# Local-plus-pooled attention and a gated feed-forward on one core: one PSUM read of h, attention groups behind the first product, second product two steps behind

## The chip, the cores and the metric

The kernel runs on one core of one Trainium2 chip. The metric is device time in microseconds (us) of one execution; the median of three runs before the change is 961.98 us (961.03 to 962.47).

## The reference, cut to what matters

For 8 batches, 8 heads, 576 positions and head size 64, two attentions are computed from q, k, v and added; the sum is the input of a feed-forward of width 512 to 2048 to 512.

```python
out_d  = softmax(scale * mean4(q) @ mean4(k).T) @ mean4(v)   # pooled by 4, 144 positions
out_up = np.repeat(out_d, 4, axis=2)
mask   = np.abs(pos[:, None] - pos[None, :]) < 4             # local band
x      = out_up + softmax(where(mask, scale * q @ k.T, -1e9)) @ v   # 4608 tokens x 512
h = x @ w_in                                                 # 512 -> 2048
g = np.where(h >= 1, h, np.where(h <= -1, 0.0, (h + 1) ** 2 / 4))
return g @ w_out                                             # 2048 -> 512
```

## The kernel before, in words

**Feed-forward.** The 4608 tokens are cut into 11 chunks: one of 512, eight of 384 (the middle chunks), two of 512. The 2048 hidden features are 16 slices of 128. A step n is one chunk and one slice (n = 16 * chunk + slice), so there are 176 steps. In each step `mm1` (L651) makes the first product: 12 matmuls (L659) into one PSUM bank `h_ps`. Each operand is split in a high and a low part (`xh`, `xl`; two planes of `w_in`), three matmuls for each of four 128-row blocks. Then `mm1` computes the activation g(h) into `u` and splits it as well: `gh` by a ScalarE cast (L683), `gl = u - gh` by GpSimd (L684). The `mm2` of a step (L687) adds the slice to the chunk's outputs: 9 matmuls (L700) into three PSUM banks `o_ps` for a middle chunk (12 into four for a chunk of 512), and copies the outputs out after slice 15 (L705, L707).

**Activation before.** In the first chunk it takes h from PSUM twice on VectorE (L672, L674). In all others ScalarE reads h (L677: relu of h/2 + 1/2), VectorE reads h (L678: max(h, 1) into `m`), ScalarE squares `u` (L679), VectorE takes the minimum (L680).

**Attention.** One unit is a pair of heads of one batch, 32 units in all. Eight of them are made before and during the first chunk by `attention` (L171). The other 24 are made in the middle chunks by the generator `join` (L393), 25 calls of it at the steps that `JOINS` lists (17, 20, 23, 26, 30, 37, 44, ... 137, 142). One call has four stages:

- stage 1, PE: the output matmuls of the unit before (L418, L433) and the scores of this unit (L447, L457), in one tile `join_ps` of four banks; SyncE issues the loads of q, k and v (L150, L156);
- stage 2: ScalarE scales the pooled output `xd` (L472); VectorE adds the band to the scores (L478) and takes maxima (L484, L495, L496, L497); GpSimd subtracts the maximum (L485); ScalarE takes exponentials of the local scores (L507) and of the three pooled blocks (L499 three times); VectorE adds local and pooled output of the unit before into `x` (L510), which ScalarE and GpSimd split into `xh`, `xl` (L379, L380);
- stage 3: VectorE sums, inverts, normalises (L522 to L528); GpSimd pools v (L535, L536); SyncE loads pooled v (L153);
- stage 4: PE transposes the weights ("the turns" below; L547 reads `sp` of L528, L553 reads `sl` of L525) into `turn_ps`, ScalarE copies them out (L557, L561), and VectorE pools the next q and k (L389), each after its load.

**Order of the work.** The code calls stages and products in program order, and a scheduler then sets a fixed order of instructions on each engine from priorities (the activation is called with a raised one, L667) and its own estimate of times. Each engine takes its own list strictly in order. In the middle chunks four banks hold `join_ps` or `turn_ps`, three hold `o_ps`, and one is left for `h_ps`: the first product of a step can start only when h of the step before has been read. `gh` and `gl` have three buffers each, `u`, `m` and the output copies share four.

Before the change a middle step n is (L725 to L735): stages 1 and 2 of a join if n is in `JOINS`, else stage 3 or 4 of the one begun a step or two ago; then mm1 of n; then mm2 of n - 1.

Of the kernel before, what the change touches and what calls it, by code (L numbers as in the profile page):

```python
# [13 lines left out]
AF = mybir.ActivationFunctionType  # L14
ALU = mybir.AluOpType
# [11 lines left out]
NFC = DFF // P  # L27
# [12 lines left out]
def ring(t):  # L40

    return (t - 512) % RING
# [60 lines left out]
JOINS = [17, 20, 23, 26, 30, 37, 44, 51, 58, 65, 69, 73, 78, 84, 91, 98, 105, 113, 117, 121, 125]  # L103
# [15 lines left out]
def attention_then_ffn(ctx: ExitStack, tc, qT, kT, vw, vp, band, w_in, w_out, out):  # L119
    nc = tc.nc  # L120
# [264 lines left out]
    def pooled_sums(n):  # L385

        state["qd"], state["kd"] = first_qd, apool.tile([P, SD], F32, name="kd", tag="kd", bufs=1)
        for t, name in ((first_qd[:, 0:SD], "q"), (state["kd"], "k")):
            nc.vector.tensor_reduce(  # L389
                t, loaded[name].rearrange("p (s f) -> p s f", f=FACTOR), axis=AX.X, op=ALU.add  # L390
            )
# [183 lines left out]
    def temp(name):  # L575
        return mpool.tile([P, 512], F32, name=name, tag="t512", bufs=4)

    def convert_weights(name, f):
# [26 lines left out]
    todo = {  # L605
        "w": iter(range(NFC)),
        "c": iter([(name, f) for f in range(NFC) for name in ("i", "o")]),
    }
    attentions = {}

    def emit(op):
        kind, n = op[0], int(op[1:] or 0)
        if kind == "a":
            if n not in attentions:
                attentions[n] = attention(n, ps_p if n < NPAIR else ps_a)
            next(attentions[n], None)
        elif kind == "c":
            convert_weights(*next(todo["c"]))
        elif kind == "w":
            load_weights(next(todo["w"]))  # L620
        elif kind == "q":
            nc.sync.dma_start(qk[n][0], qT[0, n])
            nc.sync.dma_start(qk[n][1], kT[0, n])
        elif kind == "v":
            load(0, "vp")
            load(0, "v")
        elif kind == "s":
            mm1(*next(todo["s"]))
        elif kind == "m":
            mm2(*next(todo["m"]))  # L630
# [16 lines left out]
    def turns(x):  # L647

        return x.rearrange("p (a b) -> p b a", a=2)

    def mm1(c, f):  # L651
        t0, size = CHUNKS[c]
        ts = slice(ring(t0), ring(t0) + size)
        wi = weights["i", f]
        h = places["h"].tile([P, 512], F32, name="h_ps", tag="h")[:, :size]
        n = 0
        for cc in range(NCC):
            for wt, xt in ((0, xh), (1, xh), (0, xl)):
                nc.tensor.matmul(  # L659
                    h,  # L660
                    wi[:, wt, cc * P : (cc + 1) * P],
                    turns(xt[:, cc, ts]),
                    start=(n == 0),
                    stop=(n == 3 * NCC - 1),
                )
                n += 1
        with tc.high_priority(offset=100):  # L667
            u = temp("u")[:, :size]


            if c == 0:
                nc.vector.tensor_scalar(u, h, -1.0, 1.0, op0=ALU.max, op1=ALU.add)  # L672
                nc.scalar.activation(u, u, AF.Square, scale=0.5)
                nc.vector.scalar_tensor_tensor(u, h, 1.0, u, op0=ALU.max, op1=ALU.min)  # L674
            else:
                m = temp("m")[:, :size]
                nc.scalar.activation(u, h, AF.Relu, bias=0.5, scale=0.5)  # L677
                nc.vector.tensor_scalar(m, h, 1.0, None, op0=ALU.max)  # L678
                nc.scalar.activation(u, u, AF.Square)  # L679
                nc.vector.tensor_tensor(u, u, m, op=ALU.min)  # L680
            gh = mpool.tile([P, 512], F32R, name="gh", tag="gh", bufs=3)[:, :size]
            gl = mpool.tile([P, 512], F32R, name="gl", tag="gl", bufs=3)[:, :size]
            nc.scalar.copy(gh, u)  # L683
            nc.gpsimd.tensor_tensor(gl, u, gh, op=ALU.subtract)  # L684
        gtiles[c, f] = gh, gl

    def mm2(c, f):  # L687
        t0, size = CHUNKS[c]
        gh, gl = gtiles.pop((c, f))
        if f == 0:  # L690
            otiles[c] = [
                (ps_o if t < 3 else places["o3"]).tile([P, 512], F32, name=f"o_ps{t}", tag=f"o{t}")
                for t in range(size // P)
            ]
        wo = weights["o", f]
        for t in (3, 0, 1, 2) if size == 512 else (0, 1, 2):
            o = otiles[c][t]
            ts = slice(t * P, (t + 1) * P)
            for n, (gt, wt) in enumerate(((gh, 0), (gh, 1), (gl, 0))):
                nc.tensor.matmul(  # L700
                    o, gt[:, ts], turns(wo[:, wt, :]), start=f == 0 and n == 0, stop=f == NFC - 1 and n == 2
                )
            if f == NFC - 1:
                osb = temp("osb")
                nc.scalar.copy(osb, o)  # L705
                rows = out[t0 : t0 + size, :].rearrange("(a b) d -> b a d", a=2)
                nc.sync.dma_start(rows[t * P // 2 : (t + 1) * P // 2], osb)  # L707
# [3 lines left out]
    with (  # L711
        tc.tile_pool(name="ps_o3", bufs=1, space=bass.MemoryType.PSUM) as places["o3"],
        tc.tile_pool(name="ps_h2", bufs=1, space=bass.MemoryType.PSUM) as ps_h2,
        tc.tile_pool(name="ps_a", bufs=1, space=bass.MemoryType.PSUM) as ps_a,
    ):
        places["h"] = Rotation(ps_h, ps_h2)
        for op in FIRST_STEPS:
            emit(op)
        mm1(*next(todo["s"]))
        mm2(*next(todo["m"]))  # L720
    with tc.tile_pool(name="ps_g", bufs=1, space=bass.MemoryType.PSUM) as ps_g:
        places["h"] = ps_h
        pooled_sums(SECOND)
        joined = None
        for n in range(NFC + 1, (NMID + 1) * NFC + 1):  # L725
            if n in JOINS:
                joined = join(SECOND + JOINS.index(n), ps_g)
                next(joined, None)
                next(joined, None)
            elif n - 1 in JOINS:  # L730
                next(joined, None)
            elif n - 2 in JOINS:
                next(joined, None)
            mm1(*next(todo["s"]))
            mm2(*next(todo["m"]))  # L735
    with (
        tc.tile_pool(name="ps_o3", bufs=1, space=bass.MemoryType.PSUM) as places["o3"],
        tc.tile_pool(name="ps_h2", bufs=1, space=bass.MemoryType.PSUM) as ps_h2,
# [63 lines left out]
```

## Time and profile before

| what | value |
|---|---|
| median of 3 runs | 961.98 us |
| the profiled execution's own time | 961.12 us |
| its span (first to last instruction) | 959.4 us |
| PE busy | 902.7 us, 94% |
| VectorE, ScalarE, GpSimd busy | 479.3, 473.1, 378.4 us |
| granted TensorE clock, mean | 0.982 |

The page gives busy time for each engine. PE is busy nearly throughout, but the end of a matmul is modelled, so a busy PE may still be short of work for a fraction of a microsecond. The timeline has one row for each group of like instructions: start and length in us, engine, line, operation, tiles out<-in, shape, count, and in brackets the engine's idle time before it with what ended it. A negative time below is a time ahead of the moment that is called zero there.

### The profile page before, as it was taken

The numbers are of one execution on the slowest core, as the hardware profiler recorded it, in microseconds if no ns is written. First come the engines' busy times: TensorE is split into PE (matmuls) and PEld (weight loads), VectorE is DVE, ScalarE is ACT, GpSimd is POOL, SyncE is SP. The second block draws the span as 40 slices with busy tenths as digits, with TensorE's granted clock in tenths as the row PEclk, the third lists the DMA queues.
The fourth block names the chain that finished last, engine by engine and source line by source line (L and its number), as shares of the span: only waits on it lengthen the run. The fifth ranks groups of instructions, "written<-read, shape, count | busy, mean of one in ns | idle before, by whom it ended". The sixth has DMA issues, their size and how long they took to land. (4 is left out here: it accounts for less than half of the span.)

```text
span 959.4 us, 18205 instructions
## 1 busy us (share of the span) xinstructions
PE 902.7 (94%) x7420; PEld 793.9 (83%) x7420; DVE 479.3 (50%) x836; ACT 473.1 (49%) x1011; POOL 378.4 (39%) x345
## 2 busy tenths in 40 slices
PE   4678999998999999999999999999999999999997
PEld 4556777887889888988889889988888888888886
DVE  5877797466443554355544553455556432222221
ACT  3898554445543544445444453454454443334333
POOL 2556666344443344344333443343444422222222
PEclk8689999999999999999999999999999999999999
DMA  9685110231220211132120121021231000001001
GB/s 313 223 305 206 51 53 26 72 101 52 74 63 13 72 52 52 41 88 60 51 68 18 52 84 32 21 85 52 73 115 52 15 7 27 1 1 45 1 1 44
DMA packets 26531, 66.21 MB, mean 69 GB/s; under 512 B 3152, under 2 KB 3152, under 8 KB 26448
## 3 DMA queue, kind: packets, MB, share of 16 engines
q1 hardware_dynamic: 26448, 65.06, 20.9%
q8 instruction: 58, 0.95, 0.4%
q14 instruction: 25, 0.20, 0.1%
HBM read 55.61 MB, written 9.44 MB: 68 GB/s over the span
## 5 line engine op out<-in xcount | busy, mean ns | idle before, releaser
L659 PE MATMUL h_ps<-xh,w_i 128*128 128x384 f32 (+1 forms) x1408 | 370.9, 345 | 17.2 <-DVE m L678 15.8
L684 POOL TENSOR_TENSOR gl<-u,gh 128x384 fp32r<-128x384 f32 (+1 forms) x176 | 192.2, 1092 | 452.1 <-ACT gh L683 337.8
L700 PE MATMUL o_ps<-w_o,gh 128*128 128x512 f32 x1152 | 349.5, 382 | 0.5 <-ACT gh L683 0.4
L659 PEld LDWEIGHTS h_ps<-xh,w_i 128*128 128x128 f32 x1408 | 251.7, 189 | 46.6 <-DVE m L678 25.5
L678 DVE TENSOR_SCALAR m<-h_ps 128x384 f32<-128x384 f32 (+1 forms) x160 | 93.3, 583 | 310.9 <-ACT u L677 301.9
L659 PE MATMUL h_ps<-xl,w_i 128*128 128x384 f32 (+1 forms) x704 | 240.0, 341 | 0.0
L700 PEld LDWEIGHTS o_ps<-w_o,gh 128*128 128x128 f32 x1152 | 214.5, 190 | 25.9 <-ACT gh L683 1.1
L700 PE MATMUL o_ps<-w_o,gl 128*128 128x512 f32 x576 | 220.1, 382 | 4.7 <-POOL gl L684 4.7
L677 ACT ACTIVATE u<-h_ps 128x384 f32<-128x384 f32 (+1 forms) x160 | 81.9, 512 | 225.0 <-PE h_ps L659 224.0
L683 ACT CAST gh<-u 128x384 fp32r<-128x384 f32 (+1 forms) x176 | 95.7, 544 | 107.4 <-DVE u L680 102.8
L659 PEld LDWEIGHTS h_ps<-xl,w_i 128*128 128x128 f32 x704 | 133.1, 189 | 5.4 <-issue 0.4
L700 PEld LDWEIGHTS o_ps<-w_o,gl 128*128 128x128 f32 x576 | 109.3, 190 | 22.2 <-POOL gl L684 6.9
L680 DVE TENSOR_TENSOR u<-u,m 128x384 f32<-128x384 f32 (+1 forms) x160 | 94.8, 592 | 13.6 <-ACT osb L705 0.5
L679 ACT ACTIVATE u<-u 128x384 f32<-128x384 f32 (+1 forms) x160 | 87.6, 547 | 4.7
L380 POOL TENSOR_TENSOR xl<-x,xh 128x576 fp32r<-128x576 f32 (+6 forms) x44 | 48.1, 1101 | 48.4 <-ACT xh L379 48.4
L478 DVE TENSOR_TENSOR sl<-join_ps,band_sb 128x640 f32<-128x640 f32 x24 | 19.8, 825 | 71.3 <-ACT xd L472 69.3
L485 POOL TENSOR_TENSOR sl<-sl,mxl 128x640 f32<-128x640 f32 x24 | 30.3, 1262 | 23.2 <-DVE mxl L484 23.2
L379 ACT CAST xh<-x 128x576 fp32r<-128x576 f32 (+6 forms) x44 | 23.7, 543 | 28.2 <-DVE x L510 23.7
L535 POOL TENSOR_TENSOR vh<-vp_sb 72x512 f32<-72x512 f32 x24 | 30.7, 1280 | 2.5 <-PE join_ps L433 2.5
L389 DVE TENSOR_REDUCE first_qd<-q_sb 128x144 f32<-128x576 f32 x24 | 18.1, 754 | 27.1 <-DMA q_sb<-qT 27.1
L593 POOL TENSOR_TENSOR w_i<-m,w_i 128x512 fp32r<-128x512 f32 x16 | 23.4, 1463 | 18.6 <-ACT w_i L592 18.4
L472 ACT ACTIVATE xd<-join_ps 128x144 f32<-128x144 f32 x24 | 7.0, 291 | 46.7 <-PE join_ps L457 45.8
(103 smaller groups left out, 841.7 us busy)
## 6 DMA issues: line engine op xcount, KB each, us to landing
v_sb<-vw SPq DMA_DIRECT2D x32, 320.0 KB
vp_sb<-vp SPq DMA_DIRECT2D x32, 288.0 KB
out<-osb SPq DMA_DIRECT2D x36, 256.0 KB
raw_i<-w_in SPq DMA_DIRECT2D x16, 512.0 KB
raw_o<-w_out SPq DMA_DIRECT2D x16, 512.0 KB
q_sb<-qT SPq DMA_DIRECT2D x28, 288.0 KB
k_sb<-kT SPq DMA_DIRECT2D x28, 288.0 KB
first_i<-qT SPq DMA_DIRECT2D x4, 288.0 KB
```

The lines of the kernel that those rows point to most:

```text
L379: nc.scalar.copy(xh[:, p, dst], x[:, part])
L380: nc.gpsimd.tensor_tensor(xl[:, p, dst], x[:, part], xh[:, p, dst], op=ALU.subtract)
L485: nc.gpsimd.tensor_tensor(slf, slf, ml.unsqueeze(2).broadcast_to([P, NB, WIN]), op=ALU.subtract)
L535: nc.gpsimd.tensor_tensor(vh, vpt[:, :, 0:2, :], vpt[:, :, 2:4, :], op=ALU.add)
L659: nc.tensor.matmul(h, wi[:, wt, cc * P : (cc + 1) * P], turns(xt[:, cc, ts]), start=(n == 0), stop=(n == 3 * NCC - 1),)
L677: nc.scalar.activation(u, h, AF.Relu, bias=0.5, scale=0.5)
L678: nc.vector.tensor_scalar(m, h, 1.0, None, op0=ALU.max)
L679: nc.scalar.activation(u, u, AF.Square)
L680: nc.vector.tensor_tensor(u, u, m, op=ALU.min)
L683: nc.scalar.copy(gh, u)
L684: nc.gpsimd.tensor_tensor(gl, u, gh, op=ALU.subtract)
L700: nc.tensor.matmul(o, gt[:, ts], turns(wo[:, wt, :]), start=f == 0 and n == 0, stop=f == NFC - 1 and n == 2)
```

## The change

Three things are changed, the first in `mm1`, the others in the loop over the middle steps.

- In every chunk but the first, h is read from PSUM once, by a ScalarE copy into `m`. VectorE then computes `u = max(m, -1) + 1` from SBUF, ScalarE squares u/2, and VectorE takes min(max(m, 1), u).
- In a middle step mm1 of n is called first, and the stages of a join behind it.
- mm2 is called two steps behind mm1 instead of one; step 17 has none, and one more follows the loop.

```diff
-                nc.scalar.activation(u, h, AF.Relu, bias=0.5, scale=0.5)
-                nc.vector.tensor_scalar(m, h, 1.0, None, op0=ALU.max)
-                nc.scalar.activation(u, u, AF.Square)
-                nc.vector.tensor_tensor(u, u, m, op=ALU.min)
+                nc.scalar.copy(m, h)
+                nc.vector.tensor_scalar(u, m, -1.0, 1.0, op0=ALU.max, op1=ALU.add)
+                nc.scalar.activation(u, u, AF.Square, scale=0.5)
+                nc.vector.scalar_tensor_tensor(u, m, 1.0, u, op0=ALU.max, op1=ALU.min)
...
         for n in range(NFC + 1, (NMID + 1) * NFC + 1):
+            mm1(*next(todo["s"]))
             if n in JOINS:
                 joined = join(SECOND + JOINS.index(n), ps_g)
+                next(joined)
                 next(joined, None)
+            elif n - 1 in JOINS or n - 2 in JOINS:
                 next(joined, None)
-            elif n - 1 in JOINS:
-                next(joined, None)
-            elif n - 2 in JOINS:
-                next(joined, None)
-            mm1(*next(todo["s"]))
-            mm2(*next(todo["m"]))
+            if n > NFC + 1:
+                mm2(*next(todo["m"]))
+        mm2(*next(todo["m"]))
```

The four lines of the activation keep their numbers (L677 to L680). What the scheduler makes of it is shown at the join of step 44; numbers in names tell buffers apart.

ScalarE around that join, before. `u_3487` belongs to step 44, `u_3530` to step 45:

```order
L472 ACTIVATE xd_3452<-join_ps_3395 128x144
L677 ACTIVATE u_3487<-h_ps_3474 128x384
L679 ACTIVATE u_3487<-u_3487 128x384
L507 ACTIVATE sl_3454<-sl_3454 128x640
L499 ACTIVATE sp_3459,join_ps_3395<-join_ps_3395,mxp_3460 128x144
L683 CAST gh_3493<-u_3487 128x384
L499 ACTIVATE sp_3459,join_ps_3395<-join_ps_3395,mxp_3460 128x144 x2
L379 CAST xh_80<-x_3468 128x320
L677 ACTIVATE u_3530<-h_ps_3517 128x384
```

ScalarE there now. `m_3400`, `u_3399` belong to step 44, `m_3511`, `u_3510` to step 45:

```order
L677 COPY m_3400<-h_ps_3386 128x384
L679 ACTIVATE u_3399<-u_3399 128x384
L683 CAST gh_3405<-u_3399 128x384
L472 ACTIVATE xd_3466<-join_ps_3409 128x144
L507 ACTIVATE sl_3468<-sl_3468 128x640
L499 ACTIVATE sp_3473,join_ps_3409<-join_ps_3409,mxp_3474 128x144 x2
L677 COPY m_3511<-h_ps_3497 128x384
L499 ACTIVATE sp_3473,join_ps_3409<-join_ps_3409,mxp_3474 128x144
L679 ACTIVATE u_3510<-u_3510 128x384
L379 CAST xh_80<-x_3482 128x320
```

The whole activation of step 44, its cast `gh` included, now stands ahead of `xd`, the first instruction of the join; the copy of step 45's h stands ahead of the third exponential.

VectorE from the pooling of q to the last instruction that the turns wait for (L528), before:

```order
L389 TENSOR_REDUCE first_qd_78<-q_sb_3446 128x144
L510 TENSOR_TENSOR x_3468<-join_ps_3395,xd_3452 128x576
L522 TENSOR_REDUCE join_ps_3395<-sl_3454 128x10
L389 TENSOR_REDUCE kd_3565<-k_sb_3448 128x144
L678 TENSOR_SCALAR m_3531<-h_ps_3517 128x384
L523 TENSOR_SCALAR join_ps_3395<-join_ps_3395 128x13
L680 TENSOR_TENSOR u_3530<-u_3530,m_3531 128x384
L524 RECIPROCAL join_ps_3395<-join_ps_3395 128x13
L525 TENSOR_TENSOR sl_3454<-sl_3454,join_ps_3395 128x640
L528 TENSOR_TENSOR sp_3459<-sp_3459,join_ps_3395 128x432
```

and now (`u_3553` belongs to step 46):

```order
L389 TENSOR_REDUCE first_qd_78<-q_sb_3460 128x144
L678 TENSOR_SCALAR u_3510<-m_3511 128x384
L510 TENSOR_TENSOR x_3482<-join_ps_3409,xd_3466 128x576
L680 SCALAR_TENSOR_TENSOR u_3510<-m_3511,u_3510 128x384
L522 TENSOR_REDUCE join_ps_3409<-sl_3468 128x10
L389 TENSOR_REDUCE kd_3579<-k_sb_3462 128x144
L523 TENSOR_SCALAR join_ps_3409<-join_ps_3409 128x13
L524 RECIPROCAL join_ps_3409<-join_ps_3409 128x13
L525 TENSOR_TENSOR sl_3468<-sl_3468,join_ps_3409 128x640
L678 TENSOR_SCALAR u_3553<-m_3554 128x384
L528 TENSOR_TENSOR sp_3473<-sp_3473,join_ps_3409 128x432
```

Step 45's two instructions moved forward around `x`, and the first of step 46 now stands ahead of L528.

PE at the turns of the same unit, before (the turns stand behind one matmul of mm2, step 45's):

```order
L659 MATMUL h_ps_3568<-xl_81,w_i14_1636 128x384
L700 MATMUL o_ps0_2954<-w_o13_1628,gh_3536 128x512
L547 MATMUL turn_ps_3549<-ident_67,sp_3459 72x128 x6
L553 MATMUL turn_ps_3549<-ident_67,sl_3454 128x128 x5
L700 MATMUL o_ps0_2954<-w_o13_1628,gh_3536 128x512
```

and now:

```order
L659 MATMUL h_ps_3540<-xl_81,w_i14_1636 128x384
L700 MATMUL o_ps0_2977<-w_o12_1502,gh_3405 128x512 x2
L700 MATMUL o_ps0_2977<-w_o12_1502,gl_3406 128x512
L700 MATMUL o_ps1_2978<-w_o12_1502,gh_3405 128x512 x2
L700 MATMUL o_ps1_2978<-w_o12_1502,gl_3406 128x512
L700 MATMUL o_ps2_2979<-w_o12_1502,gh_3405 128x512 x2
L547 MATMUL turn_ps_3563<-ident_67,sp_3473 72x128 x6
L553 MATMUL turn_ps_3563<-ident_67,sl_3468 128x128 x5
L700 MATMUL o_ps2_2979<-w_o12_1502,gl_3406 128x512
```

Between the end of the join's matmuls and the turns PE had the first products of three steps, the second products of two and one matmul of a third; now it has the first products of two steps, the second products of two, and 8 of 9 matmuls of a third. From the join of step 30 to that of step 133 this is so in all 19 units. In the four units before (joins 17, 20, 23, 26) the turns now stand inside a first product, behind 34 matmuls of first and 18 or 21 of second products; in the last unit (join 137) behind 24 and 22.

## What was predicted

> **What bounds the kernel now.** I read the page first, then the waits, the chain of what ended last, and the timeline of one unit of attention, since the middle steps repeat. The waits of PE in the middle and the chain's rows:
>
> ```profile
> span 959.4 us, 18205 instructions
> ...
> PE h_ps L659 <- DVE m L678: 15.8, 21, 1.7
> ...
> PE turn_ps L547 <- DVE sp L528: 1.8, 5, 0.4
> ...
> 766.41 1.94 PE o_ps L700 x9
> 768.36 1.95 PE h_ps L659 x12
> ```
>
> PE sets the end: a middle step is two blocks of 1.95 us (0.216 a matmul of the second product, 0.163 of the first). What it loses is a wait for h, once in almost every unit: 21 times, 15.8 us. PE in the unit that begins with the join of step 44:
>
> ```profile
> 306.11 0.59 PE L700 MATMUL o_ps<-w_o,gh 128*128 128x512 f32 x2
> ...
> 308.14 0.71 PE L418 MATMUL join_ps<-ap,vd 72*64 72x144 f32 x8
> ...
> 310.59 0.59 PE L659 MATMUL h_ps<-xh,w_i 128*128 128x384 f32 x2
> ...
> 319.20 0.59 PE L659 MATMUL h_ps<-xh,w_i 128*128 128x384 f32 x2 [0.55 <-DVE m L678]
> ...
> 321.49 0.82 PE L547 MATMUL turn_ps<-ident,sp 128*72 128x128 f32 x6
> ```
>
> I call the end of the join's matmuls (310.59) zero; the join took 2.5 us. The turns start at 321.49 - 310.59 = 10.90. PE's own work up to them is three first products and two second ones and one matmul: 5 x 1.95 + 0.22 = 9.97. So the unit loses 0.93 us there: the idle 0.55, some pipeline refill, and nothing to spare, because the turns wait for VectorE's L528, which ends only then. The same unit on the other engines:
>
> ```profile
> 306.31 0.49 ACT L677 ACTIVATE u<-h_ps 128x384 f32<-128x384 f32 x1 [1.48 <-PE h_ps L659]
> 306.83 0.53 ACT L679 ACTIVATE u<-u 128x384 f32<-128x384 f32 x1
> 306.90 0.56 DVE L678 TENSOR_SCALAR m<-h_ps 128x384 f32<-128x384 f32 x1 [2.67 <-ACT u L677]
> 307.56 0.56 DVE L680 TENSOR_TENSOR u<-u,m 128x384 f32<-128x384 f32 x1
> 308.21 0.51 ACT L683 CAST gh<-u 128x384 fp32r<-128x384 f32 x1 [0.86 <-DVE u L680]
> ...
> 310.70 0.29 ACT L472 ACTIVATE xd<-join_ps 128x144 f32<-128x144 f32 x1 [1.98 <-PE join_ps L457]
> 311.03 0.83 DVE L478 TENSOR_TENSOR sl<-join_ps,band_sb 128x640 f32<-128x640 f32 x1 [2.90 <-ACT xd L472]
> 311.57 0.33 SPq L150 DMA_DIRECT2D q_sb<-qT  x1
> 312.79 1.26 POOL L485 TENSOR_TENSOR sl<-sl,mxl 128x640 f32<-128x640 f32 x1 [0.93 <-DVE mxl L484]
> 314.08 0.74 ACT L507 ACTIVATE sl<-sl 128x640 f32<-128x640 f32 x1 [0.18 <-POOL sl L485]
> 314.73 0.36 ACT L499 ACTIVATE sp<-join_ps,mxp 128x144 f32<-128x144 f32 x1
> 315.04 0.52 ACT L683 CAST gh<-u 128x384 fp32r<-128x384 f32 x1
> 315.45 0.39 ACT L499 ACTIVATE sp<-join_ps,mxp 128x144 f32<-128x144 f32 x1
> 315.59 0.75 DVE L389 TENSOR_REDUCE first_qd<-q_sb 128x144 f32<-128x576 f32 x1 [0.93 <-DMA q_sb<-qT]
> 315.93 0.38 ACT L499 ACTIVATE sp<-join_ps,mxp 128x144 f32<-128x144 f32 x1
> 316.21 0.16 ACT L499 ACTIVATION_READ_ACCUMULATOR sp<-join_ps,mxp 128x1 f32 x1
> 316.41 0.76 DVE L510 TENSOR_TENSOR x<-join_ps,xd 128x576 f32<-128x576 f32 x1
> 317.20 0.83 DVE L522 TENSOR_REDUCE join_ps<-sl 128x10 f32<-128x640 f32 x1
> 317.94 0.74 DVE L389 TENSOR_REDUCE kd<-k_sb 128x144 f32<-128x576 f32 x1
> 318.60 0.55 DVE L678 TENSOR_SCALAR m<-h_ps 128x384 f32<-128x384 f32 x1
> 319.06 0.17 DVE L523 TENSOR_SCALAR join_ps<-join_ps 128x13 f32<-128x13 f32 x1
> 319.25 0.56 DVE L680 TENSOR_TENSOR u<-u,m 128x384 f32<-128x384 f32 x1
> 319.73 0.24 DVE L524 RECIPROCAL join_ps<-join_ps 128x13 f32<-128x13 f32 x1
> 320.00 0.82 DVE L525 TENSOR_TENSOR sl<-sl,join_ps 128x640 f32<-128x640 f32 x1
> 320.74 0.60 DVE L528 TENSOR_TENSOR sp<-sp,join_ps 128x432 f32<-128x432 f32 x1
> ```
>
> This is one chain: join, `xd`, L478 (it waits for `xd`), GpSimd's L485, the exponentials, then `x` at 5.82 (0.04 behind the third exponential's accumulator read, which ends at 316.37), then VectorE without a gap to 321.34, and the turns. So the question for each edit is whether it shortens this chain or the PE work beside it.
>
> **Part 1, one read of h.** Four instructions stay four, but they become serial. Before, squaring (306.83) and maximum (306.90) ran side by side, and u was done 1.81 us after the first read began (308.12). Now: copy 0.49, hand-over 0.10, L678, 0.09, square 0.53, 0.10, L680 0.56. No row shows L678 in its new form, one float source, dense, in SBUF. Its bounds: 0.17 (L523, 13 elements: the fixed cost) and 0.56 (L678 as it is, from PSUM). I take 0.36, the middle, because the nearest row, L678, has the shape and the operation but not the place of its source, and keep both ends. Then u is done after 2.23 us, 0.4 later. In plain steps that is covered: mm2 of a step now comes two steps on, and gh and gl have at least 5 us. After the last step nothing covers it: +0.4. The Trainium skill, "VectorE: DVE Perf Modes", section "The perf-mode tier table", gives a `tensor_scalar` of fp32 in SBUF twice the rate of one that reads PSUM. Halving what L678 has above the fixed cost gives 0.17 + 0.39 / 2 = 0.36, an estimate by that page; by the PSUM row alone the sum below would be +27 instead of +15; no row here settles it.
>
> What the edit removes is VectorE's read of h: mm1 two steps behind the join need no longer wait until L678 ends at 319.15, only for the copy.
>
> **Part 2, the join behind mm1.** On ScalarE, step 44's activation now stands ahead of `xd`. The join begins at -2.45 and mm1's end lies 0.09 ahead, at -2.54 (as mm2's did, whose 9 matmuls run from 306.11 to 308.05); the copy starts 0.20 later (306.31 against 306.11), at -2.34, and by the durations above ends at -1.85; L678 -1.75 to -1.39, square to -0.77, L680 to -0.11, the cast gh -0.02 to 0.49. So `xd`, which started at 0.11, starts at 0.49, and L478 at 0.82 instead of 0.44. GpSimd's L485 shifts with it to 2.58 and L507 to 3.87. Then the exponentials: first at 4.52 (+0.65, as 314.08 to 314.73), second at 5.00 (+0.48), and now the copy of the next h stands in front of the third: 5.31 (+0.31, as gh at 315.04) to 5.80. mm1 of step 46 could start at 4 x 1.95 - 1.95 = 5.85, so the old wait for h is gone. The third exponential runs from 5.80, its accumulator read ends 0.44 later, and `x` starts at 6.28 instead of 5.82. The next L678 runs at 5.90 to 6.26, just ahead of `x`. SyncE's order of loads is the same; q was issued at 0.98 and used at 5.00, which is ahead of this.
>
> From `x` on, VectorE goes by its pitches: L522's place +0.79, with L680 in front +0.48, kd +0.74, L523 +0.66, L524 +0.20, L525 +0.27, then +0.74 to the L678 of step 46, which stood behind L528 and now stands in front: +0.26 (0.36 less the overlap of 0.10 that L678 shows at 318.60 to 319.06), L528 0.60 and 0.15 to the turns: 4.89. Turns start at 6.28 + 4.89 = 11.17.
>
> **Part 3, second product two behind.** PE's work between join and turns becomes two first products, two second ones and 8 matmuls: 4 x 1.95 + 8 x 0.216 = 9.53, down from 9.97, while the turns move from 10.90 to 11.17. The loss is 1.64 instead of 0.93: +0.71 a unit. Nothing hides it: PE takes its list in order, and the rest of mm2 and the next mm1 stand behind the turns. Behind the turns ScalarE copies ap and al, 1.3 us, before the copy of the next h; PE has 2.2 us of other work, so that costs nothing.
>
> **The sum.** 19 units have this order: 19 x 0.71 = 13.5. In the last unit the turns stood 10.57 behind the join, and now behind only 24 x 0.163 + 22 x 0.216 = 8.66:
>
> ```profile
> 754.15 0.59 PE L659 MATMUL h_ps<-xh,w_i 128*128 128x384 f32 x2
> ...
> 764.72 0.49 PE L547 MATMUL turn_ps<-ident,sp 128*72 128x128 f32 x3 [0.29 <-DVE sp L528]
> ```
>
> Before, 34 and 18 matmuls (9.43) stood ahead, a loss of 1.14; now 11.17 - 8.66 = 2.51: +1.4. The first four units (steps 17 to 26) lose more before, for instance
>
> ```profile
> 217.79 0.59 PE L659 MATMUL h_ps<-xh,w_i 128*128 128x384 f32 x2 [1.69 <-DVE m L678]
> ```
>
> and their turns now stand behind 10.0 us of PE work, but more VectorE rows stand ahead of L528: I cost them at 0, between -3 and +3. Sum: 13.5 + 1.4 + 0.4 = +15.3. The profiled execution (961.12: span 959.4 and 1.7 around it) would become 976.4; the median lies 0.9 higher, 961.98 + 15.3 = 977.3, so 977.
>
> Ends: with L678 at 0.17, `xd` and `x` come 0.19 earlier and L528 0.19: turns at 10.79, loss 1.26, +0.33 a unit, in all 19 x 0.33 + 1.2 = +7.5: 969.5. At 0.56 `xd` comes 0.20 later, the next L678 ends at 6.66 and sets `x`, L528 gains 0.20 more: turns at 11.75, +1.29 a unit, 19 x 1.29 + 2.5 = +27: 989.
>
> **Rivals.** *Faster: the turns come in before PE.* If my replay of ScalarE and VectorE is too slow, the h wait goes and no other comes: at most 0.93 in 24 units = 22 us, 940. The unit breaks even at turns 0.44 earlier than before (10.46), and the whole gain needs 9.5. For it: VectorE idles 0.93 before 315.59. Against: `x` follows ScalarE's third exponential, and that gets an instruction more ahead of it. *Only the PE order counts:* cast and copy slip into gaps of ScalarE and the turns stay at 10.90: loss 1.37, +0.44 x 19 + 1 = +9, 971. *L678 stays at 0.56:* 989. *VectorE and GpSimd get in each other's way:* L680 took 0.78 us instead of 0.56 beside GpSimd's split:
>
> ```profile
> 660.31 1.15 POOL L380 TENSOR_TENSOR xl<-x,xh 128x448 fp32r<-128x448 f32 x1 [0.39 <-ACT xh L379]
> ...
> 661.09 0.78 DVE L680 TENSOR_TENSOR u<-u,m 128x384 f32<-128x384 f32 x1
> ```
>
> Step 46's L678 now falls beside such work, ahead of the turns: with 0.2 to 1.0 a unit, say 0.5, 23 x 0.5 = 12 more, 989. The Trainium skill, "SBUF — State Buffer", section "Who interferes with whom", has it that a VectorE instruction with two SBUF inputs, or one in a two-port mode, and a GpSimd one block each other for a whole instruction; the pair of rows agrees with that. *No net change:* longer chain and shorter wait cancel at turns near 10.5: 962.
>
> **How the numbers follow.** Chances: the forecast 0.44, PE order only 0.17, L678 slow 0.14, VectorE against GpSimd 0.08, no change 0.05, faster 0.12. Slower is 0.83, same 0.05, faster 0.12; 0.2% (2 us) is about what a measurement of this kernel can tell from no change. The range 965 to 992 leaves out the faster case, no change, and about 0.03 above.
>
> **What would show it.** Right: the wait of PE h_ps for VectorE is gone, and PE turn_ps L547 on L528 rises from 1.8 us to about 30, some 20 times; turns 11.2 behind the join; `xd` about 0.5 behind it with gh just ahead; L678 near 0.36. Wrong: turns under 10.5, or a wait of mm1 for ScalarE's copy as large as the old one, or losses in steps without a join.

## The result, and the profile after

The changed kernel takes 992.3 us (median of 4 runs, 991.59 to 995.82), the kernel before 961.7 us beside it. The ratio is 1.0325, with a 95% interval of 1.0299 to 1.0352: slower, by 31 us. The forecast was 977 us with a range of 965 to 992. The sign is right; the size is twice what was forecast (+30.6 instead of +15.3), and the time lies just above the range.

From the page of the changed kernel, the span (959.4 before) and PE's waits in the middle (total, times, longest):

```profile
span 989.8 us, 18135 instructions
...
PE turn_ps L547 <- ACT u L679: 20.4, 17, 1.3
...
PE h_ps L659 <- ACT m L677: 13.0, 24, 0.7
PE turn_ps L547 <- DVE sp L528: 8.0, 5, 1.9
```

Two things are to be seen. PE now waits for the turns, 22 times and 28.4 us in all, where it had waited 1.8 us. The first of the two rows names ScalarE's L679 as the releaser, since in the timeline below it ends 0.03 us behind L528 (330.12 against 330.09). But L679 writes `u`, which the turns do not read, and in all 24 units the turns start 0.14 to 0.15 us behind the end of L528, before the change as after it. So both rows are one wait, for L528. And the wait for h is still there with another name: 13.0 us behind the copy L677, where it was 15.8 us behind L678.

The unit of the join of step 44 in the timeline after (it begins at another time of the span, so only distances count; rows of several engines, in order of time):

```profile
316.22 0.48 ACT L677 COPY m<-h_ps 128x384 f32<-128x384 f32 x1 [1.25 <-PE h_ps L659]
316.80 0.36 DVE L678 TENSOR_SCALAR u<-m 128x384 f32<-128x384 f32 x1 [2.38 <-ACT m L677]
317.20 0.52 ACT L679 ACTIVATE u<-u 128x384 f32<-128x384 f32 x1 [0.50 <-DVE u L678]
317.61 1.26 POOL L535 TENSOR_TENSOR vh<-vp_sb 72x512 f32<-72x512 f32 x1 [1.51 <-PE join_ps L433]
317.75 1.54 DVE L680 SCALAR_TENSOR_TENSOR u<-m,u 128x384 f32<-128x384 f32 x1 [0.59 <-ACT u L679]
318.51 0.70 PE L700 MATMUL o_ps<-w_o,gh 128*128 128x512 f32 x2
319.33 0.51 ACT L683 CAST gh<-u 128x384 fp32r<-128x384 f32 x1 [1.61 <-DVE u L680]
319.75 0.28 ACT L472 ACTIVATE xd<-join_ps 128x144 f32<-128x144 f32 x1
320.06 0.82 DVE L478 TENSOR_TENSOR sl<-join_ps,band_sb 128x640 f32<-128x640 f32 x1 [0.77 <-ACT xd L472]
...
324.55 0.52 ACT L677 COPY m<-h_ps 128x384 f32<-128x384 f32 x1
324.95 0.39 ACT L499 ACTIVATE sp<-join_ps,mxp 128x144 f32<-128x144 f32 x1
325.12 0.59 PE L659 MATMUL h_ps<-xh,w_i 128*128 128x384 f32 x2 [0.51 <-ACT m L677]
325.44 0.75 DVE L510 TENSOR_TENSOR x<-join_ps,xd 128x576 f32<-128x576 f32 x1
...
329.22 0.35 DVE L678 TENSOR_SCALAR u<-m 128x384 f32<-128x384 f32 x1
329.49 0.60 DVE L528 TENSOR_TENSOR sp<-sp,join_ps 128x432 f32<-128x432 f32 x1
329.60 0.52 ACT L679 ACTIVATE u<-u 128x384 f32<-128x384 f32 x1 [1.75 <-DVE u L678]
330.23 0.82 PE L547 MATMUL turn_ps<-ident,sp 128*72 128x128 f32 x6 [1.17 <-ACT u L679]
```

Zero, the end of the join's matmuls, is 318.51. Up to the start of L680 the replay of the prediction holds within 0.1 us. Then one instruction breaks it: L680 takes 1.54 us instead of 0.56. It started 0.14 after GpSimd's L535, which pools v, and ended at 319.29, 0.42 behind the end of L535 (318.87). Everything behind it is late as well, by 0.75 us at first and by 0.55 at the turns. In us behind zero, from these rows:

| | forecast | after |
|---|---|---|
| L680 ends | -0.11 | 0.78 |
| `xd` starts | 0.49 | 1.24 |
| copy of the next h starts | 5.31 | 6.04 |
| `x` starts | 6.28 | 6.93 |
| turns start | 11.17 | 11.72 |

Over the whole run, the 128x384 forms of the two VectorE instructions (total, mean ns of one, idle before and its releaser):

```profile
L680 DVE SCALAR_TENSOR_TENSOR u<-m,u 128x384 f32<-128x384 f32 x128 | 91.7, 717 | 51.8 <-ACT u L679 50.4
L678 DVE TENSOR_SCALAR u<-m 128x384 f32<-128x384 f32 x128 | 48.4, 378 | 238.3 <-ACT m L677 236.5 <-DMA out<-osb 1.6
```

L678 in its new form is 0.36 to 0.38 us, as taken in the forecast. The Trainium skill, "VectorE: DVE Perf Modes", section "The perf-mode tier table", gives a `tensor_scalar` of fp32 in SBUF twice the rate of one that reads PSUM; the trace agrees: above the 0.17 of L523 it is 0.19, against 0.39 for L678 before. L680's mean is 717 ns; alone it takes 0.56 us.

One figure serves for all kernels below, the **period**: from the end of the join of step 44 to the end of that of step 51. PE's matmuls in it, seven first and seven second products of 1.95, the join (2.54) and the turns (1.14), make 31.0 us. Before it was 31.94, after 33.20 (318.51 to 351.71). Seven steps thus lost 0.94 and now lose 2.20; the same reckoning over all 24 units gives 27.5 us before and 57.6 after, so the units hold 30.1 of the 31 us.

### The profile page after: what moved, and what is told of

The parts are those of the page before. It is cut to its first block, busy times and chain, and to the rows that moved or that the text cites. A ratio compares the mean times of both kernels' runs of the same rounds, so it can differ in the third digit from the quotient of the medians.

```text
span 989.8 us, 18135 instructions
## 1 busy us (share of the span) xinstructions
PE 906.8 (92%) x7420; PEld 794.5 (80%) x7420; DVE 466.7 (47%) x836; ACT 472.3 (48%) x1011; POOL 381.7 (39%) x345
## 4 chain that ended last, share of the span: by engine, by line
PE 51%; DVE 18%; ACT 12%; issue 8%; POOL 5%; DMA 5%; SPq 0%; POOLq 0%; DVEq 0%; ACTq 0%
PE h_ps L659 24%; PE o_ps L700 22%; DVE u L680 4%; DVE u L678 2%; POOL sl L485 2%; ACT u L679 2%; DMA q_sb<-qT 2%; PE turn_ps L547 2%; ACT m L677 2%; DVE sl L478 1%; DVE mxl L484 1%; ACT sp L499 1%; DVE x L510 1%; POOL gl L684 1%; PE turn_ps L553 1%
## 5 line engine op out<-in xcount | busy, mean ns | idle before, releaser
L678 DVE TENSOR_SCALAR u<-m 128x384 f32<-128x384 f32 (+1 forms) x160 | 62.1, 388 | 347.0 <-ACT m L677 345.3
L677 ACT COPY m<-h_ps 128x384 f32<-128x384 f32 (+1 forms) x160 | 80.9, 506 | 154.1 <-PE h_ps L659 150.9
L680 DVE SCALAR_TENSOR_TENSOR u<-m,u 128x384 f32<-128x384 f32 (+1 forms) x160 | 113.9, 712 | 74.1 <-ACT u L679 72.7
L679 ACT ACTIVATE u<-u 128x384 f32<-128x384 f32 (+1 forms) x160 | 87.1, 544 | 97.7 <-DVE u L678 97.5
L507 ACT ACTIVATE sl<-sl 128x640 f32<-128x640 f32 x24 | 17.7, 739 | 67.8 <-POOL sl L485 67.8
L547 PE MATMUL turn_ps<-ident,sp 128*72 128x128 f32 x144 | 19.7, 273 | 28.4 <-ACT u L679 20.4
L547 PEld LDWEIGHTS turn_ps<-ident,sp 128*72 128x72 f32 x144 | 14.1, 115 | 36.7 <-ACT u L679 26.7
L535 POOL TENSOR_TENSOR vh<-vp_sb 72x512 f32<-72x512 f32 x24 | 30.9, 1288 | 30.6 <-PE join_ps L433 29.2
L389 DVE TENSOR_REDUCE first_qd<-q_sb 128x144 f32<-128x576 f32 x24 | 18.1, 753 | 26.9 <-DMA q_sb<-qT 26.9
```

The lines of the kernel that those rows point to most:

```text
L535: nc.gpsimd.tensor_tensor(vh, vpt[:, :, 0:2, :], vpt[:, :, 2:4, :], op=ALU.add)
L547: put(nc.tensor.transpose(tp_b[:, kb, i, :], sp[:, i, kb * KB : (kb + 1) * KB], ident if i < 2 else swapped,))
L677: nc.scalar.copy(m, h)
L678: nc.vector.tensor_scalar(u, m, -1.0, 1.0, op0=ALU.max, op1=ALU.add)
L680: nc.vector.scalar_tensor_tensor(u, m, 1.0, u, op0=ALU.max, op1=ALU.min)
```

## The experiments

The theory after the result was that of the prediction with one term put right: a unit loses what the turns start later than PE's own list of work ends, and L680 beside L535 is what made them late. Its rivals were that one of the three parts of the change costs the time by itself, and that the chain is held elsewhere. Each diff is against the changed kernel unless another is named. Each ratio is to the kernel before, run beside it on the same chip, with its 95% interval in brackets; between runs on different chips, ratios are what to compare.

### Which of the parts costs

**The new activation in the old loop** (the first hunk of the change alone).

> The new activation alone, in the old order of the loop (join, mm1, mm2 one behind). Theory (the loss of a unit is the start of its turns less PE's own work up to them; what lengthens the chain to the turns costs, what hides h costs nothing): ScalarE's square and cast of the join's step now wait for VectorE pieces that stand behind the pooling of q, and the third exponential stands behind that cast, so x starts about 7.4 us behind the join instead of 5.8 and the turns about 12.5 instead of 10.9, with PE's work unchanged at 9.98: +1.6 in some 20 units, 985 to 997 us. Rival (the order of the loop alone is what costs; a single PSUM read frees h sooner and helps): 945 to 960 us, with the wait for h gone and the turns near 10.9.

Measured: 999.7 us, ratio 1.039 (1.0353 to 1.0426), period 33.19. The single read alone costs more than the whole change. PE's waits there:

```profile
PE o_ps L700 <- ACT gh L683: 22.2, 24, 2.0
...
PE o_ps L700 <- POOL gl L684: 13.6, 28, 2.0
```

The second product, one step behind, waits for gh and gl of the step beside the join: u is a serial chain now, two of its four pieces stand in VectorE's list among the attention's, and 24 units pay up to 2 us. The turns come where the theory has them: in the unit of step 44 they start 12.13 behind the join, 0.15 behind L528's end, after a wait of 0.59. The waits there for gh (0.41) and gl (0.38) lie ahead of that, in the same stretch, so the list does not tell what each of the three is worth. The time is 3 us above the theory's range.

**The new loop with the old activation** (the second hunk alone).

> The new loop (join behind mm1, second product two behind) with the old activation. Theory: u is done 0.4 us sooner after mm1, so L680 comes ahead of GpSimd's L535 and keeps its 0.56 us, gh does not delay xd, and the scheduler puts 9.91 us of PE work ahead of the turns: turns at 11.0 to 11.4, loss 1.1 to 1.5 instead of 0.93, 964 to 974 us. Rival (the order of the loop alone is what costs): 985 us or more, turns at 11.7.

Measured: 976.5 us, 1.0147 (1.0125 to 1.017), period 32.13. That is 2 us above the expected range. In the unit of step 44 the theory holds: L680 starts 0.19 ahead of L535 (314.61 against 314.80) and keeps its 0.56, while L535 takes 1.52; `xd` starts at 0.11, the turns at 11.02. In the first experiment no L680 runs beside L535 in that unit (L680 ends at 317.48, L535 starts at 319.11). So this stretch of L680 comes with the single read and the join behind mm1 together. Some units are late for another reason than the turns. In that of step 121, VectorE and PE:

```profile
689.95 0.75 DVE L389 TENSOR_REDUCE first_qd<-q_sb 128x144 f32<-128x576 f32 x1 [3.41 <-DMA q_sb<-qT]
690.62 0.55 DVE L678 TENSOR_SCALAR m<-h_ps 128x384 f32<-128x384 f32 x1
...
691.22 0.59 PE L659 MATMUL h_ps<-xh,w_i 128*128 128x384 f32 x2 [1.62 <-DVE m L678]
```

The pooled sum of the next q waits for its load; L678 stands behind it, and so h is freed late. With the old activation, any wait in VectorE's list reaches PE through L678. The two hunks do not add up: 39 and 16 us alone, 31 together.

**The second product one step behind, the rest as changed.**

```diff
-            if n > NFC + 1:
-                mm2(*next(todo["m"]))
-        mm2(*next(todo["m"]))
+            mm2(*next(todo["m"]))
```

> The changed kernel with the second product one step behind the first instead of two; the work of TensorE between join and turns stays 9.53 us. Theory (the second step of lag hides gh and gl, which the new form makes late in the steps with attention work: the old order with the new read waited 22.2 us for gh and 13.6 us for gl): waits of 15 to 36 us for gh and gl come back, 1005 to 1028 us. Rival (the lag is not needed once the groups stand behind the first product): 986 to 998.

Measured: 999.4 us, 1.0362 (1.0338 to 1.0385), period 33.75. Both ranges missed it, the rival's by 1.4 us.

```profile
PE o_ps L700 <- POOL gl L684: 31.4, 26, 1.9
```

The waits for gl do come back, as large as expected, but the wait for the turns is gone in exchange: PE stands at gl while the chain to the turns runs on. Of 31.4 us of waiting only 4 (by the ratios) to 7 (by the times) show, and the intervals of this kernel and of the changed one overlap. Moving the join behind mm1, with the second product one step behind, can be read off in the same way: this kernel differs from the first experiment in that alone, 1.0362 against 1.039, which is not told apart.

### Where the chain to the turns is late

**The changed kernel without GpSimd's first addition** (L535; `vd` is the sum of two of four quarters).

```diff
-        vh = apool.tile([KB, NKB, 2, P], F32, name="vh", tag="al", bufs=1)
-        nc.gpsimd.tensor_tensor(vh, vpt[:, :, 0:2, :], vpt[:, :, 2:4, :], op=ALU.add)
-        nc.gpsimd.tensor_tensor(vd, vh[:, :, 0, :], vh[:, :, 1, :], op=ALU.add)
+        nc.gpsimd.tensor_tensor(vd, vpt[:, :, 0, :], vpt[:, :, 1, :], op=ALU.add)
```

> The changed kernel without GpSimd's L535 (the first of the two additions that pool v is left out, so two of four positions are summed). Theory (L680 of the join's step stretched to 1.54 us beside L535 delays gh, xd and the whole chain): L680 back at 0.56 there, xd 0.5 behind the join instead of 1.24, turns at 11.0 to 11.3 over 9.75 us of PE work, loss 1.5 instead of 2.24: 974 to 981 us. Rival (the stretch is slack that the q load or ScalarE would fill anyway): turns stay at 11.7, 987 us or more.

Measured: 1007.6 us, 1.047 (1.0439 to 1.0501): slower still, by the letter the rival's result. But the run is not a test of it, since the edit also moved another row. In the unit of step 44 (zero is 320.68):

```profile
324.98 0.75 DVE L389 TENSOR_REDUCE first_qd<-q_sb 128x144 f32<-128x576 f32 x1 [1.68 <-DMA q_sb<-qT]
325.65 0.30 DVE L496 TENSOR_REDUCE join_ps<-join_ps 128x1 f32<-128x144 f32 x1
...
326.25 0.38 ACT L499 ACTIVATE sp<-join_ps,mxp 128x144 f32<-128x144 f32 x1 [1.21 <-DVE mxp L497]
```

`xd` came early there, at 0.26, but the scheduler had put the pooled sum of q, with its wait for a load, ahead of L496 and L497; the exponentials waited for those, and the turns started at 12.06. One wait was exchanged for another. So the collision had to be tested with the place of L389 held.

**The pooled sums held behind L528, as the ground for that test.**

```diff
-            nc.vector.tensor_reduce(
+            tc.keep_in_program_order(nc.vector.tensor_reduce(
                 t, loaded[name].rearrange("p (s f) -> p s f", f=FACTOR), axis=AX.X, op=ALU.add
-            )
+            ))
```

> The changed kernel with the two pooled sums (L389) kept in program order on VectorE: they go behind L528 and the turns' step instead of between L497 and L678, and the order of TensorE then has 22 instead of 26 second products ahead of the turns (8.67 us of work instead of 9.53). It is the ground for the next run. Theory (loss of a unit = start of the turns less TensorE's own work ahead of them): VectorE's chain is about 0.8 us shorter (two sums of 0.4), the work ahead 0.86 shorter, so the loss stays near 2.2 a unit: 985 to 999 us. Rival (the wait of first_qd for its load of q is what holds the chain): the turns come over 1.5 us earlier than in the changed kernel: below 982.

Measured: 989.6 us, 1.026 (1.0241 to 1.0279), period 33.30, as the theory has it. VectorE's chain got shorter, and PE's list ahead of the turns by about as much. In its unit of step 44 (zero is 315.43):

```profile
314.54 1.29 POOL L535 TENSOR_TENSOR vh<-vp_sb 72x512 f32<-72x512 f32 x1 [1.52 <-PE join_ps L433]
314.67 1.57 DVE L680 SCALAR_TENSOR_TENSOR u<-m,u 128x384 f32<-128x384 f32 x1 [0.59 <-ACT u L679]
...
316.69 0.28 ACT L472 ACTIVATE xd<-join_ps 128x144 f32<-128x144 f32 x1
...
326.38 0.82 PE L547 MATMUL turn_ps<-ident,sp 128*72 128x128 f32 x6 [1.23 <-DVE sp L528]
```

**The same without L535** (the pooled sums held, and the edit that leaves the addition out; on PE, VectorE and ScalarE the rows stand in the same order, and from there on the lines stand two lower; only SyncE issues the load of pooled v ahead of that of v instead of behind it).

> The run before without GpSimd's first addition of the pooled v (L535); vd is the sum of the first two quarters alone, one addition instead of two. On TensorE, VectorE and ScalarE the rows stand in the same order as in the run before; on GpSimd only L535 is gone. Theory (L680 beside L535 takes 1.54 us instead of 0.56, which puts xd and the rest of the chain 0.75 to 1.0 us later): L680 is back at 0.56 in the unit, xd comes within 0.5 us of the join's end, the turns 0.7 to 1.0 earlier, over 19 to 24 units 14 to 24 us less than the run before. Rival (the chain is held elsewhere and the stretch of L680 is cover): within 6 us of the run before.

Measured: 968.0 us, 1.0045 (1.0018 to 1.0072), on the same chip as the run before and 21.6 us less. Period 32.28. Zero is 310.55, and what was L680 is L678 here:

```profile
309.80 0.56 DVE L678 SCALAR_TENSOR_TENSOR u<-m,u 128x384 f32<-128x384 f32 x1 [0.59 <-ACT u L677]
...
310.81 0.28 ACT L472 ACTIVATE xd<-join_ps 128x144 f32<-128x144 f32 x1
...
320.49 0.82 PE L545 MATMUL turn_ps<-ident,sp 128*72 128x128 f32 x6 [1.02 <-DVE sp L528]
```

L680 is back at 0.56, `xd` starts at 0.26 instead of 1.26, the turns at 9.94 instead of 10.95. The 1.0 us that L680 lost beside L535 passes through the whole chain to the turns undiminished. In this order of rows the collision costs 21.6 us, two thirds of what the change lost. The wait for h behind the copy, 11.2 us in the run before, is gone as well, since the copy stands in ScalarE's list behind the same `xd`.

**The whole computation, with L535 moved instead of left out** (the pooled sums held, and L535 kept in program order, which puts it behind xl and the next gl).

```diff
-        nc.gpsimd.tensor_tensor(vh, vpt[:, :, 0:2, :], vpt[:, :, 2:4, :], op=ALU.add)
+        tc.keep_in_program_order(nc.gpsimd.tensor_tensor(vh, vpt[:, :, 0:2, :], vpt[:, :, 2:4, :], op=ALU.add))
```

> The changed kernel with the sums pinned and L535, L536 kept in program order, the turns where the change has them: the run that left L535 out, but with the whole computation. Theory (the price is the place of L535, not its being there): as without L535, 964 to 974 us. Rival (in its new place it stretches L680, L678 or the split of x as much): 982 or more.

Measured: 964.4 us, 1.0003 (0.9986 to 1.0021), period 32.29: as without L535. TensorE, VectorE and ScalarE keep the order of rows of the run with the sums held; GpSimd's order differs by L535, and SyncE's order of issues in places. It is the place of L535 that costs, not the work.

### Whether the turns are what PE waits for

**The changed kernel with the turns one step later.**

```diff
-            elif n - 1 in JOINS or n - 2 in JOINS:
+            elif n - 1 in JOINS or n - (2 if n < 26 else 3) in JOINS:
```

> The changed kernel with stage 4 (the turns) called one step later from step 26 on, so that 11.71 us of PE work stand ahead of the turns instead of 9.53. Theory (PE only waits because it comes to the turns too early): the wait at the turns goes in 20 units, only the wait of about 0.5 us for the copy of h is left, loss about 0.7 instead of 2.24: 958 to 967 us. Rival (VectorE and ScalarE cannot carry the work of a unit in time, the wait moves to the next join or to h): 980 us or more.

Measured: 968.2 us, 1.007 (1.0048 to 1.0092), period 31.90, a shade above the expected range. PE has 11.71 us of its own work ahead of the turns instead of 9.53, and the wait at the turns of the ordinary units is gone, and with it 24 us of the 31 (PE waits 6.4 us there, 4 times, instead of 28.4). What is left in a unit, 0.9 us, is the wait for h behind the copy, 13.0 us in all as in the changed kernel, with what PE loses around it.

**The same edit in the kernel before.**

> The kernel before with nothing but the turns one step later from step 26 on. Theory (before, a unit loses its 0.9 us at the wait for h, which VectorE's second read L678 frees late, and the turns only came in together with it): 955 to 965 us, no gain worth the name. Rival (the turns' chain was the bound): 20 units x 0.9 us go, 940 to 950.

Measured: 962.3 us, 0.9981 (0.9963 to 0.9998), period 31.92 against 31.94. As expected, next to nothing: before, a unit lost its 0.94 us at h, and the turns only came in together with it.

```profile
PE h_ps L659 <- DVE m L678: 16.9, 22, 1.9
```

**The same edit in the new loop with the old activation.**

> The new order of the loop and the lag of two, with the old activation, and from step 26 on the turns one step later (11.71 us of TensorE's work between join and turns instead of 9.91). Theory: without the late turns the turns came 11.0 us behind the join in most units, which the longer work now covers, so 0.9 to 1.1 us of loss goes in 20 units, and half of the longer ones: 18 to 24 us below the 976.5 of the order alone, 951 to 960, and faster than before. Rival (what the turns feed comes too late, so that h, xl or the next join waits instead): 964 or more.

Measured: 974.4 us, 1.0102 (1.0071 to 1.0133), period 31.93: a miss of 14 us, and the rival is right.

```profile
PE h_ps L659 <- DVE m L678: 20.5, 18, 3.2
```

With the turns out of the way, the wait for VectorE's read of h takes their place (14.4 us with the turns early). So the late turns alone gain 2.5% where h is read once (1.0325 to 1.007), and where it is read twice no gain is told apart (1.0147 to 1.0102, with intervals that overlap).

### Putting them together

**Pooled sums held and turns late.**

> The changed kernel with both edits that runs before had alone: the pooled sums (L389) kept behind L528, and the turns one step later from step 26 on (11.71 us of TensorE's work between join and turns). Theory (loss of a unit = what comes last of the turns' chain and the waits for h): the 1.27 us of wait at the turns of 22 units (27.9 us in all) go, the waits for h of about 0.5 stay: 962 to 972 us. Rival (what stands behind the turns becomes late in their place, as with the old activation): 978 or more.

Measured: 960.5 us, 0.996 (0.9942 to 0.9978), period 31.90. Below the expected range by 1.5 us.

**The same with L535 kept in program order:** all three edits, the whole computation.

> The run before (sums pinned, late turns) with GpSimd's additions of the pooled v (L535, L536) kept in program order: they come behind xl and the next step's gl instead of beside the L680 at the join; nothing is left out, and VectorE's rows stand in the same order. Theory (beside L535 L680 takes 1.54 us and shifts xd, the exponentials and with them the copy of the next h, for which TensorE still waits): the waits for h go as well, 8 to 18 us less than the run before, 946 to 962, faster than the kernel before the change. Rival (with the turns late the chain has room, and the collision costs nothing any more, or moves to another L678 or L680): within 4 us of the run before.

Measured: 942.7 us, 0.9779 (0.9741 to 0.9817), period 31.10, 17.8 us less than the run before it on the same chip, and 2.2% faster than the kernel before the change. The difference is at the upper end of the forecast (8 to 18); the time itself lies 3 us below the range of 946 to 962. The unit of step 44 (zero is 305.76):

```profile
305.00 0.56 DVE L680 SCALAR_TENSOR_TENSOR u<-m,u 128x384 f32<-128x384 f32 x1 [0.59 <-ACT u L679]
...
306.01 0.28 ACT L472 ACTIVATE xd<-join_ps 128x144 f32<-128x144 f32 x1
...
315.47 0.35 DVE L678 TENSOR_SCALAR u<-m 128x384 f32<-128x384 f32 x1
315.51 1.47 POOL L535 TENSOR_TENSOR vh<-vp_sb 72x512 f32<-72x512 f32 x1
315.86 0.52 ACT L679 ACTIVATE u<-u 128x384 f32<-128x384 f32 x1 [1.53 <-DVE u L678]
316.41 0.98 DVE L680 SCALAR_TENSOR_TENSOR u<-m,u 128x384 f32<-128x384 f32 x1 [0.59 <-ACT u L679]
...
317.54 0.82 PE L547 MATMUL turn_ps<-ident,sp 128*72 128x128 f32 x6
...
318.02 1.01 POOL L684 TENSOR_TENSOR gl<-u,gh 128x384 fp32r<-128x384 f32 x1
318.43 0.82 DVE L678 TENSOR_SCALAR u<-m 128x384 f32<-128x384 f32 x1 [1.03 <-ACT m L677]
```

PE no longer waits in this unit: 31.10 against 31.0 of work. The collision has not gone; L535 now meets a later L680 (0.98) and gl an L678 (0.82). But these stand in steps whose u is wanted two steps on, with nothing behind them that the turns of this unit wait for, and there they cost nothing that the period shows.

**The same with the old activation** (the first hunk of the change undone).

> The fastest kernel so far (new loop, sums pinned, turns one step later, L535 behind xl and gl) with the old activation: h read by ScalarE and, in L678, by VectorE. Theory (the single read is worth the wait for h that it takes away: with the old form h of the step after the join comes free only when VectorE reaches L678, which stands among x, L522 and L528): waits for h of 0.4 to 1.0 a unit come back, 952 to 964 us. Rival (the order alone does it, the read costs and brings nothing): 938 to 947.

Measured: 954.0 us, 0.9902 (0.9871 to 0.9933), period 31.73. In the unit of step 44 (the rows of VectorE and PE):

```profile
318.19 0.55 DVE L678 TENSOR_SCALAR m<-h_ps 128x384 f32<-128x384 f32 x1
...
318.80 0.59 PE L659 MATMUL h_ps<-xh,w_i 128*128 128x384 f32 x2
```

L678 ends at 318.74 and mm1 starts 0.06 behind it. Twice a unit mm1 comes some 0.2 us late in this way and its second matmul 0.1 later than elsewhere, too short for the list of waits, 0.6 a unit in all, as the theory has it. So in this kernel the single read is worth 1.2% (0.9779 against 0.9902), where in the change it cost 1.8% (1.0325 against 1.0147).

**The three edits in the kernel before.**

> The kernel before, its loop and activation as they were, with the same three edits (sums pinned, turns one step later, L535 kept in program order). Theory (its loss is the wait for h behind L678, which none of the three moves): 952 to 965 us. Rival (the three edits help any loop, and the change isn't needed for the gain): 938 to 948.

Measured: 969.4 us, 1.0066 (1.0043 to 1.009), period 32.09. No gain: 4 us above the theory's range and far from the rival's. But the theory's reason fails. The wait for h behind L678 has shrunk to 4.8 us, from 15.8, and the second product, one step behind the first here, waits for gl instead:

```profile
PE o_ps L700 <- POOL gl L684: 12.7, 26, 2.0
```

In the unit of step 44 the split xl on GpSimd (from 316.63) gets in ahead of an L680, and the gl of that step comes late:

```profile
316.72 1.26 DVE L680 TENSOR_TENSOR u<-u,m 128x384 f32<-128x384 f32 x1
...
319.65 0.48 PE L700 MATMUL o_ps<-w_o,gl 128*128 128x512 f32 x1 [0.34 <-POOL gl L684]
```

So the three edits pay in the loop of the change and not in the old one.

## Why the prediction was right and wrong

**What bounds the kernel.** Right that PE's list is the bound and that a unit loses what comes late to it. "Nothing to spare, because the turns wait for L528" was half the truth: before, h alone set the 0.94, and the turns moved a step later left the time where it was.

**Part 1, the single read.** The size of L678 was right (0.36). "The old wait for h is gone" failed: it was 13.0 us instead of 15.8, since in the unit of step 44 the copy starts at 6.04 and not at 5.31. The step itself was sound: without the collision, no wait for h is left in these units (the runs without L535 and with L535 moved).

**Part 2, the join behind mm1.** This is the step that failed. The forecast laid L680 at -0.67 to -0.11 with its bare 0.56 and looked there only at VectorE's and ScalarE's queues. GpSimd's L535 is released by the join's L433, at the same moment; it got in first by 0.14 us, and L680 ended 0.42 behind it. So L680 ended 0.89 later than forecast, `xd` started 0.75 later, and 0.55 of it are left at the turns. L535 waits for L433 because its output `vh` takes the buffer of `al` (both have the tag "al", with one buffer), which L433 reads. Before the change it already ran around the end of the join, from -0.83 to 0.46:

```profile
309.76 1.29 POOL L535 TENSOR_TENSOR vh<-vp_sb 72x512 f32<-72x512 f32 x1
```

The forecast laid L680 inside that span. That the collision costs its full length is shown where the pooled sums are held; in the changed kernel's own order the 0.55 at the turns is read from the timeline.

**Part 3 and the sum.** The loss per unit was set at 9.53 of work against turns at 11.17, 1.64; they came at 11.72, 2.19. By units: the 19 like that of step 44 lost 23.7 us more than before, forecast 13.5; the first four lost 5.1 more, costed at 0; the last 1.1, forecast 1.4. The 10 and the 5 are the whole miss of 15. In the first four a collision of the same kind was left out: in the unit of step 23 the split xl holds up an L678 ahead of the turns, which takes 1.12 us instead of 0.35,

```profile
220.75 1.41 POOL L380 TENSOR_TENSOR xl<-x,xh 128x576 fp32r<-128x576 f32 x1
221.25 1.12 DVE L678 TENSOR_SCALAR u<-m 128x384 f32<-128x384 f32 x1
...
224.73 0.82 PE L547 MATMUL turn_ps<-ident,sp 128*72 128x128 f32 x6 [1.88 <-DVE sp L528]
```

and an L678 and an L680 now stand between the pooled sum, which waits for its load of q (2.51 us, 2.22 before), and `x`, which starts 7.63 behind the join instead of 6.96 (219.07 and, before, 215.01). How the 5.1 split between these was not measured.

**The rivals.** "VectorE and GpSimd get in each other's way" was the right mechanism and nearly the right time (989), with a chance of 0.08 and at the wrong place: at step 46's L678, which ran at its 0.35, instead of at the join's L680. The Trainium skill, "SBUF — State Buffer", section "Who interferes with whom", says that a VectorE instruction with two SBUF inputs contends with a GpSimd instruction that reads SBUF, and that the port pair they share is an exclusive lock. The trace agrees: L680 ended 0.42 behind the end of L535, and taken as running only after L535, its end would have come out within 0.15 us. The chance should have come from asking which GpSimd row starts within the span of each VectorE row on the chain, and the answer stood in the rows of the join.

**What stays open.** The units of steps 30 and 78 still lose 1.4 us in the fastest kernel and the first four up to 1.7; no run went after these. Nor did one part the new loop under the three edits: whether they need the join behind mm1, the second step of lag, or both is not shown; the wait for gl in the old loop speaks for the lag.

## What to carry to other kernels

An instruction that is moved gets new neighbours on the other engines: for each VectorE instruction that lies on the chain, look up what GpSimd runs at its new time, and above all what the same event releases. A wait list shows one wait of several that overlap: take away the largest and see which takes its place before the part is called dear or cheap. Here the single read cost 1.8% where the collision and the early turns bound, and was worth 1.2% where they did not.

## What the runs showed of the hardware

- The stretch is a wait, not a slower rate. L680 (two SBUF inputs, 128x384, 0.56 alone) ended 0.42 us behind the end of L535 after a start 0.14 behind it (1.54), 0.41 in the run with the sums held (1.57), and again 0.41 when it started 0.90 behind it (0.98). Where L680 got in first, by 0.19, it kept its 0.56 and L535 took 1.52 instead of 1.26 (the new loop with the old activation).
- L678 with one SBUF input does the same behind gl: 0.82 instead of 0.36, ended 0.22 behind gl's end (319.25 against 319.03). Started 0.04 ahead of L535 it kept its 0.35, and L535 took 1.47 instead of 1.26 (the spans of GpSimd are rough).
- PE pays a little more after a wait: where mm1 had waited for h (314.60 in the run with all three edits and the old activation), its third matmul started 0.42 us behind the first, and 0.32 in the steady part of the same block (315.19 to 315.51).
